# Order of the first loads in a fused attention and expert-routing kernel: first v between the k loads, blank rows in nine parts, constants in parts, rank products after the transposes

## The chip, the cores and the metric

The kernel runs on one core of a Trainium2 chip. The core has five engines with a queue of instructions each: TensorE (PE, matrix products; its weight loads are listed as PEld), VectorE (DVE), ScalarE (ACT), GpSimd (POOL) and SyncE (SP). SP only issues transfers. POOL computes and issues transfers as well. All transfers run on the core's 16 DMA engines.

The metric is the device time of one execution in microseconds (us), as a median over runs. About 0.5% (3.4 us) is what a measurement of this kernel can tell from no change.

## The reference: what is computed

Two blocks follow each other. The first is attention inside chunks of 64 positions:

```python
batch, n_heads, seq, head_dim = (8, 8, 576, 64)      # q, k, v, float32
chunk = 64
scores = scale * np.matmul(q_c, k_c.transpose(0, 1, 2, 4, 3))   # per chunk, 64 x 64
scores = scores - np.max(scores, axis=-1, keepdims=True)
attn = np.exp(scores)
attn = attn / (np.sum(attn, axis=-1, keepdims=True) + 1e-09)
out = np.matmul(attn, v_c)
```

Its output, with the heads side by side, is x: 4608 tokens of 512 numbers. The second block sends every token to one of 8 experts:

```python
logits = xn @ en.T / tau              # x and expert_emb by their norms
expert_idx = np.argmax(logits, axis=1)
gate_w = softmax(logits)[n, expert_idx[n]]
h = np.maximum(x[mask] @ w1[e], 0.0)             # w1: 8 x 512 x 1024
out[mask] = gate_w[mask, None] * (h @ w2[e])     # w2: 8 x 1024 x 512
```

## The kernel before

**Attention stage.** The 4608 tokens are 36 tiles of 128 (two chunks each). A batch of the input has 9 chunks, so it covers four and a half tiles. For each tile the kernel loads k and q (`load_qk`, line 572: `kx`, `qx`, 256 KB each), transposes them on PE (`turn_qk`, line 595), forms the scores (`scores`, line 611; DVE takes the maximum and subtracts it, lines 619 and 621), takes exp on ACT (`weights`, line 631), transposes the result (`turn_a`, line 637), and multiplies by v (`values`, line 651, tile `pv`; DVE divides by the sums, lines 659 to 662, into the row buffer `xr`, which has eight places). `turn_x` (line 680) transposes the tile's x for the router.

v is loaded by batch, with one transfer per head (`load_v`, line 584). Two buffers take turns, and `values(t)` of tile 4 is the first that reads batch 1. Chunks 0 to 3 and 4 to 8 of batch 0 are two separate calls.

**Router.** After every four tiles PE forms the logits (`logits`, line 695), transposes them back (`copy_logits`, line 710), and DVE picks the expert (`pick`, lines 724 to 728, result `eqb_all`). `place` (from line 737) counts with a few small products on PE how many earlier tokens chose the same expert (the "rank products"), and DVE makes of that a row number `dest` (lines 762 to 771). `put` (line 800) then writes a tile's rows by an indirect transfer, issued on POOL, into the table `spots` in memory. In `spots` every expert has a region; the first 4 groups of 64 rows of the first and the last expert's regions are read early, before all places are known, so they are first filled with rows that count as empty: `clear_first` (lines 549 to 556) copies the tile `blank` there.

**Expert stage.** From some 200 us on, the kernel reads groups of rows from `spots`, and PE multiplies them with w1 and w2 (lines 253, 342, 413).

**What sets the order.** The order is written out by hand: a loop over t from -3 to 38 (line 1024) works on several tiles at once, `turn_qk(t + 3)`, `scores(t + 2)`, `turn_x(t - 1)`, `values(t)`, and `load_qk(t + 7)`. Each engine executes its instructions in that order. k and q have four buffers each. k of the first four tiles is loaded on SP, all other k and all q on POOL; v and the blank rows on SP. In the built program, transfers on SP use eight completion counters in turn, so each transfer there also waits until the one eight places before it has finished. The `constants` (lines 509 to 547) are some forty small POOL instructions, all issued at the end of t = 0; `clear_first` follows at the end of t = 1, and the load of v's batch 1 in t = 2:

```python
                b = (2 * t + 2) // NCB + 1
                if b not in v_t and b < B and t > 1:
                    load_v(b)
```

Of the kernel before, what the change touches and what calls it, by code (L numbers as in the profile page):

```python
# [11 lines left out]
I32 = mybir.dt.int32  # L12
AF = mybir.ActivationFunctionType
ALU = mybir.AluOpType
# [7 lines left out]
NO_ROW = 200000  # L22
# [3 lines left out]
def kernel(  # L26
# [11 lines left out]
    nc = tc.nc  # L38
    B, H, S, Dh = q.shape
    E, D = moe_expert_emb.shape  # L40
# [13 lines left out]
    NE = 4  # L54
# [115 lines left out]
    def first_rows(s, j, n):  # L170
        r0 = (0, E - 1)[s] * R + G * j
        return spots[r0 : r0 + G * n, :]
# [273 lines left out]
    with (  # L446
# [59 lines left out]
        in_g = one.tile([P, 1], FP32, name="in_g")  # L506
        e_p = one.tile([P, 1], FP32, name="e_p")

        def constants():
            nc.gpsimd.iota(io_i, pattern=[[1, NST]], base=0, channel_multiplier=0)  # L510
            nc.gpsimd.iota(part_i, pattern=[[0, 1]], base=0, channel_multiplier=1)
            make_upper_triangular(nc, sltb, val=1.0, diag=False)
            nc.gpsimd.memset(onesb, 1.0)
            nc.gpsimd.memset(blank, 0.0)
            nc.gpsimd.memset(blank[:, D + TOK : D + TOK + 1].bitcast(I32), NO_ROW)
            nc.gpsimd.memset(ones, 1.0)
            nc.gpsimd.memset(before, 0.0)
            nc.gpsimd.memset(eqb_all[:, 0], 0.0)
            nc.gpsimd.memset(jump[:, 1], 1.0)
            nc.gpsimd.memset(nb[:, 0:1], float((SPARE + R) // G))  # L520
            nc.gpsimd.tensor_copy(io, io_i)
            nc.gpsimd.tensor_copy(at, part_i)
            nc.gpsimd.tensor_scalar(pref, io[:, 0:E], -1.0, float(E), ALU.mult, ALU.add)
            nc.gpsimd.tensor_scalar(e_base, io[:, 0:E], float(R), None, ALU.mult)
            nc.gpsimd.tensor_scalar(second, at, float(G), None, ALU.is_ge)
            nc.gpsimd.tensor_scalar(is_0, at, 2.0, None, ALU.is_lt)
            nc.gpsimd.tensor_scalar(lim, at, -float(P), float(G * NE), ALU.mult, ALU.add)
            nc.gpsimd.tensor_scalar(step, second, -2.0, 1.0, ALU.mult, ALU.add)
            nc.gpsimd.tensor_scalar(first_s, second, -1.0, 1.0, ALU.mult, ALU.add)
            nc.gpsimd.tensor_scalar(back, io, -1.0, float(NST - 1), ALU.mult, ALU.add)  # L530
            nc.gpsimd.tensor_scalar(more_g, back, float(LEAST - NE), None, ALU.is_ge)
            nc.gpsimd.tensor_scalar(pair_g, back, float(LEAST - NE), None, ALU.is_equal)
            nc.gpsimd.tensor_tensor(more_g, more_g, pair_g, ALU.add)
            nc.gpsimd.tensor_tensor(pair_g, back, more_g, ALU.subtract)
            nc.gpsimd.memset(more_e[:, NSW - 1 : NSW], 1)
            nc.gpsimd.tensor_scalar(e_0, second, float(E - 1), None, ALU.mult)
            nc.gpsimd.tensor_scalar(e_1, e_0, 1.0, None, ALU.add)
            nc.gpsimd.tensor_scalar(ends_e, io[:, 0:E], 0.0, None, ALU.is_equal)
            nc.gpsimd.tensor_scalar(full, io[:, 0:E], float(E - 1), None, ALU.is_equal)
            nc.gpsimd.tensor_tensor(ends_e, ends_e, full, ALU.add)  # L540
            nc.gpsimd.tensor_scalar(done, ends_e, float(NE), None, ALU.mult)
            nc.gpsimd.tensor_scalar(ends_e, ends_e, is_0, None, ALU.mult)
            nc.gpsimd.tensor_scalar(in_g, second, -float(G), at, ALU.mult, ALU.add)
            nc.gpsimd.tensor_scalar(e_p, second, float(R), None, ALU.mult)
            nc.gpsimd.tensor_scalar(
                base_h, io[:, 0 : E // 2], 2.0 * R, e_p, ALU.mult, ALU.add
            )

        def clear_first():

            for s in range(2):
                nc.sync.dma_start(
                    out=first_rows(s, 0, NE).rearrange("(j p) w -> p j w", p=G),
                    in_=blank[0:G].unsqueeze(1).to_broadcast([G, NE, W]),
                )
            nc.sync.dma_start(out=spots[SPARE : SPARE + G, :], in_=blank[0:G])

        before = one.tile([P, E], BF16, name="before")
# [2 lines left out]
        def load_qk(t):  # L561

            for src, nm, eng in (
                (k, "kx", nc.sync if t < 4 else nc.gpsimd),
                (q, "qx", nc.gpsimd),
            ):
                x = qk_p.tile([P, H, Dh], FP32, tag=nm, name=nm)
                done = 0
                while done < P:
                    b, s = divmod(t * P + done, S)  # L570
                    n = min(P - done, S - s)
                    eng.dma_start(  # L572
                        out=x[done : done + n],
                        in_=src[b, :, s : s + n, :].rearrange("h p d -> p h d"),
                    )
                    done += n
                qk_t[nm, t] = x.rearrange("p h d -> p (h d)")

        def load_v(b, c0=0, c1=NCB, eng=nc.sync):

            t = v_sb[b % 2]
            for h in range(H):
                r0 = CH * (h % 2)
                eng.dma_start(
                    out=t[r0 : r0 + CH, h // 2, c0:c1, 0:Dh],
                    in_=v[b, h].rearrange("(c k) d -> k c d", k=CH)[:, c0:c1],
                )
            v_t[b] = t
# [87 lines left out]
        def turn_x(t):  # L676
            d = st[t]
            ps = ps_t.tile([P, KD, P], FP32, tag="tr", name="tr")
            for c in range(KD):
                nc.tensor.transpose(ps[:, c], d["x"][:, c * P : c * P + P], ident)  # L680
            xT = wk.tile([P, KD, P], FP32, tag="xT", name="xT", bufs=RB + 1)
            nc.scalar.copy(xT, ps)  # L682
            d["xT"] = xT
            junk = one.tile([P, D], FP32, tag="junk", name="junk")
            nc.scalar.activation(
                junk, d["x"], AF.Square, accum_out=xr[:, t % NX, D + SQ : D + SQ + 1]
            )
# [20 lines left out]
        def copy_logits(b):  # L708
            n, t = sizes[b], sum(sizes[:b])
            nc.tensor.transpose(lt_ps, copied[b], ident)  # L710
            copied[b] = xr[:, t % NX : t % NX + n, D : D + E]
            nc.vector.tensor_copy(
                copied[b], lt_ps.rearrange("p (n e) -> p n e", e=Q)[:, 0:n, 0:E]
            )
# [278 lines left out]
        load_qk(1)  # L993
        for x in v_sb:
            nc.vector.memset(x[:, :, :, Dh : Dh + 1], 1.0)
        load_qk(2)
        load_qk(3)
        load_v(0, 0, 4)
        load_v(0, 4, NCB)
        norm_experts()  # L1000
        nc.gpsimd.memset(xr[:, :, D:W], 0.0)

# [18 lines left out]

        early_t = 26
        ends = {sum(sizes[: b + 1]) - 1: b for b in range(len(sizes))}
        for t in range(-3, NT + 3):

            if 0 <= t < NT:
                turn_a(t)
            if t == early_t - 1:
                count_early()
            if t + 3 < NT:  # L1030
                turn_qk(t + 3)
                if t + 7 < NT:
                    load_qk(t + 7)
            if t - 2 in ends:
                logits(ends[t - 2])
            if t == NT:
                turn_x(t - 1)
            early_parts(t, 0)
            if 0 <= t + 2 < NT:
                scores(t + 2)  # L1040
            if t - 2 in ends:
                copy_logits(ends[t - 2])
            if t - 3 in ends:
                place(ends[t - 3])
            if 0 <= t - 1 < NT - 1:
                turn_x(t - 1)
            if 0 <= t < NT:
                values(t)
                b = (2 * t + 2) // NCB + 1
                if b not in v_t and b < B and t > 1:  # L1050
                    load_v(b)
            if t == NT - 8:
                load_first(w1_sb, w1_rows)
            if t == NT - 6:
                load_first([w[0] for w in w2_sb], w2_rows)
            if 0 <= t + 2 < NT:
# [12 lines left out]
            early_parts(t, 1)  # L1069
            if t == -2:  # L1070
                turn_experts()
            if t == 0:
                constants()
            if t == 1:
                clear_first()
        groups()
        pad_places()
        put(len(to_put))
# [148 lines left out]
```

## Time and profile before

| | us |
|---|---|
| median of nine runs | 687.15 (681.52 to 690.77) |
| the profiled execution | 685.52 |
| its span | 683.7 |

| engine | busy us | share of the span |
|---|---|---|
| PE | 628.7 | 92% |
| DVE | 421.3 | 62% |
| ACT | 445.4 | 65% |
| POOL | 155.5 | 23% |

The profile is of one execution. A busy share is a mean over stages with different limits, so what a part of the kernel is worth is read from the stretch where it runs. A line of a timeline gives the start, the duration, the engine, the line of the kernel, the operation with its output and inputs, the number of instructions merged, and in brackets how long the engine had been idle before and what ended that. "issue" is a wait for nothing that the profile shows. A line of waits gives the total, how often, and the longest. A line of a stretch gives the busy time of PE, PEld, DVE, ACT and POOL (with their instructions), PE's granted clock as a share of full speed, the mean busy share of the 16 DMA engines and the rate.

Times of the product with v (`pv`, line 651) by tile: 0 at 16.34, 1 at 20.92, 2 at 24.21, 3 at 28.71, 4 at 32.01, 5 at 46.75, 6 at 50.61, 7 at 54.21, 8 at 57.87, 9 at 62.73, 11 at 70.90.

### The profile page before, as it was taken

The numbers are of one execution on the slowest core, as the hardware profiler recorded it, in microseconds if no ns is written. First come the engines' busy times: TensorE is split into PE (matmuls) and PEld (weight loads), VectorE is DVE, ScalarE is ACT, GpSimd is POOL, SyncE is SP. The second block draws the span as 40 slices with busy tenths as digits, with TensorE's granted clock in tenths as the row PEclk, the third lists the DMA queues.
The fourth block names the chain that finished last, engine by engine and source line by source line (L and its number), as shares of the span: only waits on it lengthen the run. The fifth ranks groups of instructions, "written<-read, shape, count | busy, mean of one in ns | idle before, by whom it ended". The sixth has DMA issues, their size and how long they took to land. (4 is left out here: it accounts for less than half of the span.)

```text
span 683.7 us, 24844 instructions
## 1 busy us (share of the span) xinstructions
PE 628.7 (92%) x9744; PEld 342.3 (50%) x9744; DVE 421.3 (62%) x1140; ACT 445.4 (65%) x776; POOL 155.5 (23%) x237
## 2 busy tenths in 40 slices
PE   6869898798779999999999999989999999999993
PEld 5657777686424544544544444334444444444441
DVE  4738788788369664565676556777565567564430
ACT  4626666575222767767787776878877767877650
POOL 7827676743140100100010010000100000100101
PEclk9979999999989999999999999999999999999997
DMA  9978998888936811111778111775831114411101
GB/s 258 258 185 237 256 258 263 231 245 327 343 106 227 340 57 45 49 39 44 277 261 313 49 49 41 270 290 175 331 110 42 49 46 159 172 42 33 49 30 34
DMA packets 94590, 112.66 MB, mean 165 GB/s; under 512 B 52364, under 2 KB 72588, under 8 KB 94456
## 3 DMA queue, kind: packets, MB, share of 16 engines
q1 hardware_dynamic: 82728, 72.84, 33.3%
q0 software_dynamic: 11696, 38.04, 16.8%
q8 instruction: 81, 1.33, 0.8%
q14 instruction: 53, 0.43, 0.2%
q10 hardware_dynamic: 32, 0.02, 0.0%
HBM read 334.71 MB, written 22.69 MB: 523 GB/s over the span
## 5 line engine op out<-in xcount | busy, mean ns | idle before, releaser
L413 PE MATMUL y_ps<-w,hT 128*32 128x512 f32 (+1 forms) x2368 | 272.8, 589 | 0.0
L361 ACT ACTIVATE h<-C 64x256 f32<-64x256 f32 x264 | 178.3, 675 | 95.7 <-DVE C L374 69.1
L413 PEld LDWEIGHTS y_ps<-w,hT 128*32 128x32 f32 x2368 | 87.2, 110 | 157.5 <-issue 147.4
L428 POOL DMA_INDIRECT out_dram<-y,spot x36 | 34.9, 971 | 438.0 <-ACT y L421 209.8
L374 DVE TENSOR_TENSOR C<-C,h 128x256 f32<-128x256 f32 x231 | 96.0, 416 | 49.3 <-DVEq L299 42.5
L342 PE MATMUL h<-w,S 128*32 128x256 f32 x1056 | 95.9, 379 | 0.0
L342 PE MATMUL h<-sums,xbT 128*32 128x256 f32 x1056 | 95.2, 379 | 0.0
L342 PE MATMUL h<-w,xbT 128*32 128x256 f32 x1056 | 78.6, 380 | 7.2 <-ACTq L299 6.0
L368 DVE STREAM_TRANSPOSE hT<-h 128x512 f32<-128x512 f32 x66 | 46.7, 708 | 44.0 <-ACT h L361 43.9
L342 PEld LDWEIGHTS h<-w,xbT 128*32 128x32 f32 x1056 | 40.6, 110 | 43.3 <-ACTq L299 13.4
L342 PEld LDWEIGHTS h<-w,S 128*32 128x32 f32 x1056 | 48.8, 110 | 21.8 <-ACT w L301 0.4
L342 PEld LDWEIGHTS h<-sums,xbT 128*32 128x32 f32 x1056 | 48.3, 110 | 21.9 <-ACT C L377 0.4
L227 DVE TENSOR_SCALAR rn<-rn 128x1 f32<-128x1 f32 x37 | 5.7, 153 | 68.6 <-ACT rn L224 68.6
L342 PE MATMUL h<-sums,S 128*32 128x256 f32 x528 | 47.9, 379 | 0.0
L800 POOL DMA_INDIRECT spots<-xr,dest x36 | 37.1, 1030 | 38.8 <-DVE dest L765 11.3
L682 ACT COPY xT<-tr 128x512 f32<-128x512 f32 x36 | 21.1, 587 | 37.7 <-PE tr L680 37.7
L203 DVE STREAM_TRANSPOSE xbT<-xin 128x256 f32<-128x256 f32 x73 | 44.4, 645 | 0.5 <-DVE hT L368 0.5
L224 ACT ACT_TABLE_LOAD x34 | 43.6, 1283 | 1.0 <-issue 0.3
L231 ACT ACT_TABLE_LOAD x34 | 43.6, 1283 | 0.6
L421 ACT ACTIVATE y<-y_ps,gate 128x512 f32<-128x512 f32 (+1 forms) x37 | 25.2, 682 | 24.6 <-issue 8.8
L572 POOL DMA_DIRECT2D kx<-in_k_dram x36 | 31.4, 875 | 20.7 <-PE tr L595 20.7
L651 PE MATMUL pv<-v,aT 64*64 64x65 f32 x1152 | 28.1, 227 | 8.1 <-DMA v<-in_v_dram 5.4
(202 smaller groups left out, 811.5 us busy)
## 6 DMA issues: line engine op xcount, KB each, us to landing
w<-in_moe_w_dram SPq DMA_DIRECT2D x74, 2048.0 KB
next_w<-in_moe_w_dram SPq DMA_DIRECT2D x67, 2048.0 KB
xin<-spots SPq DMA_DIRECT2D x158, 64.0 KB
qx<-in_q_dram POOLq DMA_DIRECT2D x32, 256.0 KB
v<-in_v_dram SPq DMA_DIRECT2D x56, 144.0 KB
kx<-in_k_dram POOLq DMA_DIRECT2D x28, 256.0 KB
spot<-spots SPq DMA_DIRECT2D x80, 4.0 KB
spots<-blank SPq DMA_DIRECT2D x2, 576.0 KB
```

What stands on the lines that cost most here:

```text
L203: nc.vector.transpose(xT[:, :, cols].rearrange("p c (b i) -> p b c i", i=Q), t[:, s * (D // 2) : (s + 1) * (D // 2)].rearrange("p (b i c) ...
L224: nc.scalar.activation(rn, spot[:, j % SPOTS, SQ : SQ + 1], AF.Sqrt)
L231: nc.scalar.activation(sh, sh, AF.Exp, accum_out=gate)
L342: nc.tensor.matmul(ps[t0 : t0 + Q], lhsT=a[:, c, s], rhs=w[:, r], start=c == 0, stop=c == KD // 2 - 1,)
L361: nc.scalar.activation(h[b][G * v : G * v + G, s].rearrange("p (k i) -> p k i", i=Q), x[G * s : G * s + G].rearrange("p (i k) -> p k i", i=Q),
L368: nc.vector.transpose(hT.rearrange("p k (s b i) -> p b s k i", b=2, i=Q)[:, b], h[b].rearrange("p s (k i) -> p s k i", i=Q),)
L374: nc.vector.tensor_tensor(out, a, b, op)
L413: nc.tensor.matmul(ps[Q * r : Q * r + Q, 0:w], lhsT=d["hT"][:, c, Q * t0 : Q * t0 + Q], rhs=w2_sb[s][buf_of(j)][:, c, d0 : d0 + w], start= ...
L428: ins = nc.gpsimd.indirect_dma_start(out=to, out_offset=bass.IndirectOffsetOnAxis(ap=at, axis=0), in_=y[:, 0:w], in_offset=None, bounds_ch ...
L572: eng.dma_start(out=x[done : done + n], in_=src[b, :, s : s + n, :].rearrange("h p d -> p h d"),)
L651: nc.tensor.matmul(pv[CH * c : CH * c + CH, par, i], lhsT=d["aT"][r0 : r0 + CH, i, CH * c : CH * c + CH], rhs=v_t[b][r0 : r0 + CH, i, cb, ...
L800: ins = nc.gpsimd.indirect_dma_start(out=spots, out_offset=bass.IndirectOffsetOnAxis(ap=at, axis=0), in_=m, in_offset=None, bounds_check=S ...
```

## The change

- **First loads on SP.** Before: k of tiles 0 to 3, then v's batch 0 (sixteen transfers). After: k of tiles 0 and 1, the first eight transfers of v, k of tiles 2 and 3, and then, in t = -2, the other eight of v. q stays on POOL.
- **Blank rows.** Before: two transfers of 576 KB and one of 144 KB, together. After: nine of 144 KB each, two at the end of each of t = 1 to 4 and one in t = 5.
- **v's batch 1.** It is loaded at the end of t = 1, behind two blank transfers, where it stood behind all of them. On SP the order is then: two blanks, batch 1, four blanks, batch 2 (which waits for tile 4's product), three blanks, batch 3.
- **Constants.** The same instructions, in fifteen parts, one at the end of each of t = 0 to 14; `blank` is written in the first part.
- **Rank products.** `place` is called after `turn_x(t - 1)` where it was called before it. On PE the four transposes of x now stand ahead of the rank products, once in four tiles. On DVE and ACT nothing moves.

```diff
-        def constants():
+        def constant_parts():
             nc.gpsimd.iota(io_i, pattern=[[1, NST]], base=0, channel_multiplier=0)
             nc.gpsimd.iota(part_i, pattern=[[0, 1]], base=0, channel_multiplier=1)
+            nc.gpsimd.memset(blank, 0.0)
+            nc.gpsimd.memset(blank[:, D + TOK : D + TOK + 1].bitcast(I32), NO_ROW)
+            yield
             make_upper_triangular(nc, sltb, val=1.0, diag=False)
             nc.gpsimd.memset(onesb, 1.0)
-            nc.gpsimd.memset(blank, 0.0)
-            nc.gpsimd.memset(blank[:, D + TOK : D + TOK + 1].bitcast(I32), NO_ROW)
...
+            yield
             nc.gpsimd.tensor_scalar(second, at, float(G), None, ALU.is_ge)
             nc.gpsimd.tensor_scalar(is_0, at, 2.0, None, ALU.is_lt)
+            yield
...
         def clear_first():
 
-            for s in range(2):
-                nc.sync.dma_start(
-                    out=first_rows(s, 0, NE).rearrange("(j p) w -> p j w", p=G),
-                    in_=blank[0:G].unsqueeze(1).to_broadcast([G, NE, W]),
-                )
+            for j in range(NE):
+                for s in range(2):
+                    nc.sync.dma_start(out=first_rows(s, j, 1), in_=blank[0:G])
+                    yield
             nc.sync.dma_start(out=spots[SPARE : SPARE + G, :], in_=blank[0:G])
...
         load_qk(1)
         for x in v_sb:
             nc.vector.memset(x[:, :, :, Dh : Dh + 1], 1.0)
+        load_v(0, 0, 4)
         load_qk(2)
         load_qk(3)
-        load_v(0, 0, 4)
-        load_v(0, 4, NCB)
         norm_experts()
...
+        constants, clears = constant_parts(), clear_first()
         for t in range(-3, NT + 3):
...
+            if t == -2:
+                load_v(0, 4, NCB)
             if t - 2 in ends:
                 logits(ends[t - 2])
...
+            if 0 <= t - 1 < NT - 1:
+                turn_x(t - 1)
             if t - 3 in ends:
                 place(ends[t - 3])
-            if 0 <= t - 1 < NT - 1:
-                turn_x(t - 1)
             if 0 <= t < NT:
                 values(t)
...
-            if t == 0:
-                constants()
+            if t >= 0:
+                next(constants, None)
+            if t >= 1:
+                next(clears, None)
+                next(clears, None)
             if t == 1:
-                clear_first()
+                load_v(1)
```

More of the change, by code (lines that the diff above doesn't have):

```diff
@@ L507 @@
         e_p = one.tile([P, 1], FP32, name="e_p")
-        def constants():
+        def constant_parts():
             nc.gpsimd.iota(io_i, pattern=[[1, NST]], base=0, channel_multiplier=0)
             nc.gpsimd.iota(part_i, pattern=[[0, 1]], base=0, channel_multiplier=1)
+            nc.gpsimd.memset(blank, 0.0)
+            nc.gpsimd.memset(blank[:, D + TOK : D + TOK + 1].bitcast(I32), NO_ROW)
+            yield
             make_upper_triangular(nc, sltb, val=1.0, diag=False)
             nc.gpsimd.memset(onesb, 1.0)
-            nc.gpsimd.memset(blank, 0.0)
-            nc.gpsimd.memset(blank[:, D + TOK : D + TOK + 1].bitcast(I32), NO_ROW)
-            nc.gpsimd.memset(ones, 1.0)
+            nc.gpsimd.tensor_copy(io, io_i)
+            nc.gpsimd.tensor_copy(at, part_i)
+            yield
+            nc.gpsimd.tensor_scalar(pref, io[:, 0:E], -1.0, float(E), ALU.mult, ALU.add)
+            nc.gpsimd.tensor_scalar(e_base, io[:, 0:E], float(R), None, ALU.mult)
@@ L517, in constants @@
             nc.gpsimd.memset(before, 0.0)
             nc.gpsimd.memset(eqb_all[:, 0], 0.0)
+            nc.gpsimd.memset(ones, 1.0)
+            yield
             nc.gpsimd.memset(jump[:, 1], 1.0)
             nc.gpsimd.memset(nb[:, 0:1], float((SPARE + R) // G))
[L521 to L524, printed above, removed]
+            yield
@@ L525, in constants @@
             nc.gpsimd.tensor_scalar(second, at, float(G), None, ALU.is_ge)
             nc.gpsimd.tensor_scalar(is_0, at, 2.0, None, ALU.is_lt)
+            yield
             nc.gpsimd.tensor_scalar(lim, at, -float(P), float(G * NE), ALU.mult, ALU.add)
             nc.gpsimd.tensor_scalar(step, second, -2.0, 1.0, ALU.mult, ALU.add)
+            yield
             nc.gpsimd.tensor_scalar(first_s, second, -1.0, 1.0, ALU.mult, ALU.add)
             nc.gpsimd.tensor_scalar(back, io, -1.0, float(NST - 1), ALU.mult, ALU.add)
+            yield
@@ L531, in constants @@
             nc.gpsimd.tensor_scalar(more_g, back, float(LEAST - NE), None, ALU.is_ge)
             nc.gpsimd.tensor_scalar(pair_g, back, float(LEAST - NE), None, ALU.is_equal)
+            yield
             nc.gpsimd.tensor_tensor(more_g, more_g, pair_g, ALU.add)
             nc.gpsimd.tensor_tensor(pair_g, back, more_g, ALU.subtract)
+            yield
             nc.gpsimd.memset(more_e[:, NSW - 1 : NSW], 1)
             nc.gpsimd.tensor_scalar(e_0, second, float(E - 1), None, ALU.mult)
+            yield
@@ L537, in constants @@
             nc.gpsimd.tensor_scalar(e_1, e_0, 1.0, None, ALU.add)
             nc.gpsimd.tensor_scalar(ends_e, io[:, 0:E], 0.0, None, ALU.is_equal)
+            yield
             nc.gpsimd.tensor_scalar(full, io[:, 0:E], float(E - 1), None, ALU.is_equal)
             nc.gpsimd.tensor_tensor(ends_e, ends_e, full, ALU.add)
+            yield
             nc.gpsimd.tensor_scalar(done, ends_e, float(NE), None, ALU.mult)
             nc.gpsimd.tensor_scalar(ends_e, ends_e, is_0, None, ALU.mult)
+            yield
@@ L543, in constants @@
             nc.gpsimd.tensor_scalar(in_g, second, -float(G), at, ALU.mult, ALU.add)
             nc.gpsimd.tensor_scalar(e_p, second, float(R), None, ALU.mult)
+            yield
             nc.gpsimd.tensor_scalar(
@@ L549, in clear_first @@
         def clear_first():
[L551 to L555 removed]
+            for j in range(NE):
+                for s in range(2):
+                    nc.sync.dma_start(out=first_rows(s, j, 1), in_=blank[0:G])
+                    yield
             nc.sync.dma_start(out=spots[SPARE : SPARE + G, :], in_=blank[0:G])
```

## The prediction

> **What bounds the kernel now.** I read the page first: span 683.7 us, TensorE (PE) busy 92% of it.
>
> ```profile
> span 683.7 us, 24844 instructions
> PE   6869898798779999999999999989999999999993
> ...
> PEclk9979999999989999999999999999999999999997
> DMA  9978998888936811111778111775831114411101
> ```
>
> A slice is 17.1 us. From slice 13 on PE is full at full clock: the expert stage, which the change does not touch. The first eleven slices (to 188 us) are attention, where PE and the transfers are both near full. One slice stands out, the third (34 to 51 us): PE 6, clock 7. So I went to the waits up to 180 us (total, times, longest):
>
> ```profile
> POOL kx L572 <- PE tr L595: 20.7, 10, 9.8
> ...
> DVE rs L659 <- PE pv L651: 13.1, 3, 8.2
> ACT aT L639 <- PE tr L637: 12.9, 3, 8.5
> ...
> PE pv L651 <- DMA v<-in_v_dram: 5.4, 4, 3.5
> ```
>
> Three engines wait 8 to 10 us once, and PE waits for v. The timelines say where: PE, then SP's own issues.
>
> ```profile
> 32.01 0.45 PE L651 MATMUL pv<-v,aT 64*64 64x65 f32 x12
> 33.32 0.58 PE L651 MATMUL pv<-v,aT 64*64 64x65 f32 x6 [0.85 <-issue]
> 34.96 0.48 PE L651 MATMUL pv<-v,aT 64*64 64x65 f32 x4 [1.07 <-DMA v<-in_v_dram]
> 35.63 0.48 PE L651 MATMUL pv<-v,aT 64*64 64x65 f32 x4 [0.18 <-DMA v<-in_v_dram]
> 39.66 0.48 PE L651 MATMUL pv<-v,aT 64*64 64x65 f32 x4 [3.55 <-DMA v<-in_v_dram]
> 40.76 0.48 PE L651 MATMUL pv<-v,aT 64*64 64x65 f32 x2 [0.62 <-DMA v<-in_v_dram]
> 41.17 1.11 PE L637 MATMUL tr<-ident,a 128*128 128x128 f32 x4
> ```
> ```profile
> 18.78 1.31 SPq L552 DMA_DIRECT2D spots<-blank  x2
> 20.14 2.24 SPq L556 DMA_DIRECT2D spots<-blank  x1
> 22.42 44.25 SPq L584 DMA_DIRECT2D v<-in_v_dram  x24
> ```
>
> The stalled product is tile 4's, the first to read batch 1 of v. That load stands on SP behind three blank writes (576, 576, 144 KB). In the built program a DMA on SP also waits for the one eight places before it, so the last three v loads wait for the blank writes to finish. Issued alone, the eighth starts at 30.31 and runs 2.54; its product went at 40.76. The transfers were full meanwhile (the last three columns of a stretch are PE's clock, the busy share of the DMA engines, and GB/s):
>
> ```profile
> 20.00:24.00 4.00, 3.08 (x79) 2.78 (x79) 2.62 (x6) 2.54 (x6) 3.38 (x16) 1.00 0.97 233
> 24.00:28.00 4.00, 3.12 (x79) 2.57 (x77) 2.81 (x6) 2.69 (x6) 3.43 (x10) 1.00 0.91 204
> ...
> 36.00:40.00 4.00, 0.45 (x6) 0.29 (x4) 0.00 (x0) 0.00 (x0) 0.00 (x0) 0.50 1.06 265
> ```
>
> The blank writes went first, and then v had to share with q and k of tiles 8 to 11, all issued from 25.95 on, because GpSimd (POOL) had run constants from 17.14 to 25.76.
>
> **Part 1: v's batch 1 ahead of most blank writes.** Tile 4's product starts at 32.01, tile 7's at 54.21: 22.20 us. The same four-tile stretch one batch later runs 57.87 to 70.90 (13.03), then 13.25, 13.18, 13.09: mean 13.14. So the stall, with the half clock after it (a transpose group 1.11 against 0.66), is worth 22.20 - 13.14 = **9.06 us** at most.
>
> Does v arrive? After the change SP has two blank writes (0.29 MB) and then v (1.18 MB). Blank is written on POOL right after the tile number at 17.06, so near 18.1; at 0.65 us an issue, six v loads follow by about 23.4 and the last two wait for the two blank writes. Behind the queue at the start, a v load issued 3.79 to 6.14 let its successor (eight places on) go at 11.18: 5 us from issue to landing; by that row the last v lands near 25.2 + 5 = 30. By bytes: the trace moves about 290 GB/s there; in 25.5 to 40.7 us SP's ring got about 1.6 MB (v's batch 1, 1.18 MB, and three loads of batch 2) while POOL's had 2.1 MB (tiles 8 to 11): a share of 43%, 0.125 MB/us. 1.47 MB from 18.2 us take 11.8: 30.0 us. Both come 2 us before tile 4 asks (32.01). I take no wait here, and 3 us as the far end: one load as slow as the one issued at 36.85 (3.54 us against 0.6).
>
> A rule against that: the Trainium skill, "DMA: Bandwidth & Descriptors", section "Rules for kernel authors", says to coalesce and gives 1 MiB a transfer for bandwidth; its "Anatomy" section has about 2.0 us fixed plus bytes over 436 GB/s for one DMA. If the pieces ran one after the other, my estimate from that page is nine of 2.3 us against 9 us for the three: 12 us more of SP's queue. The trace's own row is different: sixteen v loads of 64 and 80 KB went out 0.6 us apart and overlapped, at 246 to 339 GB/s in all. By the row the splitting costs six more issues, 6 x 0.65 = 3.9 us of SP.
>
> Those 3.9 us lie where SP has nothing else due: SP is idle from 43.15 to 58.24. If that cover goes, batch 2 of v is late; it is issued once tile 4 is done (33) and needed at tile 9 (62.73 now, some 54 then). With 0.59 MB of blank before it at 0.125 MB/us it lands by 44 to 46. Cost nothing, bounds 0 to 1.
>
> **Part 2: k of tiles 2 and 3 behind eight v loads (a loss).** Now tile 2's k goes out at 1.87 and its transposes run at 10.63. Then it waits behind two k and eight v issues: about 2 x 0.55 + 8 x 0.62, one of them waiting for a v: issue near 7.0. By bytes SP's ring must deliver 1.31 MB, with POOL's even share 2.6 MB in all; the windows give 2.34 MB at 10 and 2.88 at 12 us: 11.0. By the 5 us row: 12.5 to 13. PE then waits 0.4 to 2.4 us at 10.63; below nothing is excluded, since no k can be earlier than it is. PE was at half speed till 14.4 (1.06 a group); if the gap puts that off, 1.7 more. I take 1.2, bounds 0 to 4. The Trainium skill ("TensorE: Matmul & The Clock Gate", "Why this matters for your kernels") puts the gap that cools PE above about 3 us; by it the 1.7 falls away. Tile 3's k (12.9 by bytes) is due at 14.40, and v's first half, now early, was never waited for (its product waited 0.28 for ACT).
>
> **Part 3: constants in parts.** POOL's 8.6 us block goes into tiles 0 to 14 at 0.2 to 1.2 us each; POOL is busy 3.1 of some 4.2 us a tile with puts. Tile 8's k goes out near 18.5 instead of 25.95; it competes with v, as counted above. No reader is early: the first (pref, tile 5) is written in tile 2. Cost 0, bounds -0.5 to +1.
>
> **Part 4: rank products behind the transposes of x.** PE idles before L737 for 0.40 to 1.83 us in a batch:
>
> ```profile
> 66.55 0.18 PE L737 MATMUL rt_ps<-eqb_all,sltb 128*128 128x32 bf16 x1 [1.04 <-DVE eqb_all L728]
> ...
> 66.68 0.64 PE L680 MATMUL tr<-ident,xr 128*128 128x128 f32 x4
> ...
> 70.34 0.63 PE L680 MATMUL tr<-ident,xr 128*128 128x128 f32 x4 [0.32 <-issue]
> ```
>
> The 0.54 us of transposes would fill the wait, but DVE runs without a gap from 66.42 to 70.20, and the next tile's transposes (70.34) follow its last result. What is saved is lost there. I take 0; bounds -4.3 (0.54 in eight batches) and +0.5.
>
> **Part 5: the last blank writes.** Three of the nine stand behind v's batch 2, issued about 33 to 40, so out by 42 and landed by 45 to 48. The first put waits for all of them; it would be due at 53.25 - 9 = 44. POOL is in order, so tile 14's k waits too, but it has three tiles of lead. Taken: 0.4, bounds 0 to 2.
>
> **Sum.** -9.06 + 0 + 0 + 1.2 + 0 + 0 + 0.4 = -7.5 us. The profiled execution took 685.52 (span 683.7 and 1.8 around it): 678.0. The median of nine runs is 687.15, 1.6 above it: 679.6.
>
> **Rivals.**
> *Transfers bind.* Bytes are conserved: the ring was full during the stall, and afterwards (48 to 56 us) it fell to 0.33 and 0.35, which shows spare time that the change would use. For it: share 0.9 to 1.1 nearly everywhere; from 18.5 us to tile 9 (54) there are 0.6 MB left over, 4.7 of q and k (tiles 8 to 16), 1.3 of blanks, 2.4 of v and 1.2 of puts, 10.2 MB or 35 us at 290 GB/s, for 35 us. Against: 2.1 MB of these (tiles 13 to 16) are prefetch, and no k or q wait shows after 6.29 us. Half of the stall would return: 684.
> *The rank move counts.* If DVE's chain loosens, the 4.3 us come on top: 675.5.
> *Slower.* The first put. A tile's row buffer is rewritten eight tiles later, and 3.5 us pass between a put and its release (145.56 to 149.03). Tile 8 then needs its row at about 50.7, so the put may go at 47.2 at the latest. Each us that the ninth blank lands later is lost, and beyond about 47.2 + 7.9 = 55 us the kernel is slower. For it: three blanks behind eight loads that wait for PE. Against: landing estimated at 45 to 48. With landing at 60: 692.
> *Nothing happens.* v lands when it did, since bytes and not order decide: then 687 plus part 2, 688. Against: the three waits for finished blank writes.
>
> **How the numbers follow.** As summed 0.60; transfers bind 0.15; rank counts 0.10; slower 0.10; nothing happens 0.05. About 0.5% (3.4 us) is what a measurement can tell from no change. Predicted 679.6. The range takes in the rank case below, with half a microsecond more, 675.0, and above it the ends of parts 2 and 5 (2.8 and 1.6 over what I took) and the half stall: 685.5. What is left out is the slower case, that of nothing, and the far edge of the others, 0.2 together. Faster by over 0.5% (under 683.7): the sum's case, the rank case and a third of the transfers' case: 0.75. Within 0.5%: the rest of that case, and nothing (688): 0.15. Slower: 0.10.
>
> **What the profile after would show.** Right: no wait over 1 us at the product of tile 4, clock 1.00 from 32 to 46 us, tile 7's product near 46, everything later shifted by the same. Part 2: a wait of PE for k at about 10.6. Part 4: the wait before L737 shorter, the one before the next transposes as long. Wrong if PE's wait for v stands at tile 4 or comes back at tile 9, if POOL waits for blank writes beyond 48 us, or if "issue" waits of PE grow while transfers are full from 18 to 50 us.

## The result, and the profile after

| | us |
|---|---|
| before, median | 688.21 (681.52 to 692.3) |
| changed kernel, median | 681.3 (676.0 to 687.1) |
| ratio | 0.9896 (0.9871 to 0.992) |
| forecast | 679.6, a ratio of 0.989 |

The ratio, here and in the tables below, is estimated from fast runs alone (a run can fall into a slower state), and it differs from the quotient of the two medians by up to 0.2%.

The changed kernel is 1.0% faster, some 7 us. Its profiled execution took 676.73 us with a span of 675.0, against 685.52 and 683.7; it lies 4.6 us under its median, that of before 2.7 under its own, so the two profiles are 8.7 us apart. The page of it, to set beside the page of before:

```profile
span 675.0 us, 24854 instructions
...
PE   5989998987789999999999999999999999999993
...
PEclk9989999999989999999999999999999999999998
DMA  9989899979817711111787111776821114511101
```

The weak third slice is gone: PE 8 and clock 8 where 6 and 7 stood. The first slice is weaker, 5 for 6. The waits of the first 180 us (total, times, longest) name the same groups as before; the lines moved by 13 in the code:

```profile
POOL kx L585 <- PE tr L608: 17.0, 8, 5.5
...
DVE rs L672 <- PE pv L664: 7.3, 3, 3.9
PE tr L608 <- DMA kx<-in_k_dram: 6.7, 2, 3.9
```

The longest waits of POOL and DVE are about half of what they were. Below that in the list stands `PE pv L664 <- DMA v<-in_v_dram: 3.1, 4, 1.3`: PE still waits for v. The timelines of PE, and of SP's issues, show where:

```profile
13.26 0.84 PE L608 MATMUL tr<-ident,kx 128*128 128x128 f32 x4 [2.75 <-DMA kx<-in_k_dram]
...
31.88 0.56 PE L664 MATMUL pv<-v,aT 64*64 64x65 f32 x18
32.60 0.33 PE L664 MATMUL pv<-v,aT 64*64 64x65 f32 x4 [0.17 <-DMA v<-in_v_dram]
33.49 0.33 PE L664 MATMUL pv<-v,aT 64*64 64x65 f32 x4 [0.55 <-DMA v<-in_v_dram]
35.12 0.33 PE L664 MATMUL pv<-v,aT 64*64 64x65 f32 x4 [1.30 <-DMA v<-in_v_dram]
36.49 0.33 PE L664 MATMUL pv<-v,aT 64*64 64x65 f32 x2 [1.03 <-DMA v<-in_v_dram]
```
```profile
7.52 2.21 SPq L585 DMA_DIRECT2D kx<-in_k_dram  x2
9.77 6.62 SPq L597 DMA_DIRECT2D v<-in_v_dram  x8
20.61 1.19 SPq L567 DMA_DIRECT2D spots<-blank  x2
21.84 9.64 SPq L597 DMA_DIRECT2D v<-in_v_dram  x8
31.52 2.58 SPq L567 DMA_DIRECT2D spots<-blank  x4
34.20 6.73 SPq L597 DMA_DIRECT2D v<-in_v_dram  x8
40.98 1.54 SPq L567 DMA_DIRECT2D spots<-blank  x2
42.56 0.62 SPq L569 DMA_DIRECT2D spots<-blank  x1
```

Tile 4's product starts when it did, 31.88 against 32.01, and waits 3.05 us for v in four pieces instead of 5.4. The wait for the k of tile 2 at 13.26 is new.

Where the 8.7 us between the two spans lie, by the starts of the product with v:

| stretch | before | after | difference |
|---|---|---|---|
| start to tile 4 | 32.01 | 31.88 | -0.13 (tile 0 +2.34, regained by tile 3) |
| tile 4 to 7 | 22.20 | 17.68 | -4.52 |
| tile 7 to 24 | 70.50 | 69.04 | -1.46 |
| tile 24 to 35 | 48.00 | 44.07 | -3.93 |
| tile 35 to the end | 511.0 | 512.3 | +1.34 |

So only half of the 8.7 us lies where the prediction put it. The rest lies further on, where of the change only the rank products and, up to tile 14, the constants are left, and the experiments had to say whether it belongs to the change at all.

### The profile page after: what moved, and what is told of

Its sections match the earlier page's. It is cut to its first block, busy times and chain, and to the rows that moved or that the text cites. A ratio compares the mean times of both kernels' runs of the same rounds, so it can differ in the third digit from the quotient of the medians.

```text
span 675.0 us, 24854 instructions
## 1 busy us (share of the span) xinstructions
PE 625.5 (93%) x9744; PEld 355.6 (53%) x9744; DVE 422.8 (63%) x1140; ACT 445.5 (66%) x776; POOL 157.3 (23%) x237
## 3 DMA queue, kind: packets, MB, share of 16 engines
HBM read 334.71 MB, written 22.69 MB: 530 GB/s over the span
## 5 line engine op out<-in xcount | busy, mean ns | idle before, releaser
L413 PE MATMUL y_ps<-w,hT 128*32 128x512 f32 (+1 forms) x2368 | 269.1, 589 | 0.0
L413 PEld LDWEIGHTS y_ps<-w,hT 128*32 128x32 f32 x2368 | 90.1, 110 | 152.6 <-issue 145.7
L342 PE MATMUL h<-w,S 128*32 128x256 f32 x1056 | 89.5, 379 | 0.0
L342 PE MATMUL h<-sums,xbT 128*32 128x256 f32 x1056 | 89.0, 379 | 0.0
L342 PE MATMUL h<-w,xbT 128*32 128x256 f32 x1056 | 75.4, 380 | 7.2 <-ACTq L299 6.0
L203 DVE STREAM_TRANSPOSE xbT<-xin 128x256 f32<-128x256 f32 x73 | 46.1, 669 | 0.5 <-DVE hT L368 0.5
L342 PE MATMUL h<-sums,S 128*32 128x256 f32 x528 | 44.7, 379 | 0.0
L421 ACT ACTIVATE y<-y_ps,gate 128x512 f32<-128x512 f32 (+1 forms) x37 | 25.2, 681 | 22.6 <-issue 8.8
L585 POOL DMA_DIRECT2D kx<-in_k_dram x36 | 32.0, 890 | 18.1 <-PE tr L608 17.0
L585 POOL DMA_DIRECT2D qx<-in_q_dram x40 | 34.4, 865 | 0.9 <-PE tr L608 0.4
```

The source lines that it names most:

```text
L203: nc.vector.transpose(xT[:, :, cols].rearrange("p c (b i) -> p b c i", i=Q), t[:, s * (D // 2) : (s + 1) * (D // 2)].rearrange("p (b i c) ...
L342: nc.tensor.matmul(ps[t0 : t0 + Q], lhsT=a[:, c, s], rhs=w[:, r], start=c == 0, stop=c == KD // 2 - 1,)
L413: nc.tensor.matmul(ps[Q * r : Q * r + Q, 0:w], lhsT=d["hT"][:, c, Q * t0 : Q * t0 + Q], rhs=w2_sb[s][buf_of(j)][:, c, d0 : d0 + w], start= ...
L421: nc.scalar.activation(y[:, 0:w], ps[:, 0:w], AF.Copy, scale=gate_of.pop(j))
L585: eng.dma_start(out=x[done : done + n], in_=src[b, :, s : s + n, :].rearrange("h p d -> p h d"),)
```

## Experiments

Four theories run through the expectations. A: the place in SP's queue makes tile 4 wait, DVE's chain takes back what the rank products save, and the early delay is regained. B: the transfers bind, and bytes set the time. C: half of the gain is the stall, the new order of the first loads costs some 3 us, and the rank products give 2 to 4. D, formed on the results of the second group: a gain at tile 4 lasts only where the first put need not wait for blank rows. The kernels of a group below ran on one chip, beside the kernel before on that chip, which took 676.79, 675.95 and 676.65 us on these three, where it took 688 for the result.

**One part at a time (first chip).**

`v1_ahead`: the kernel before, with batch 1 of v ahead of all blank rows, and nothing else.

```diff
             if t == 1:
+                load_v(1)
                 clear_first()
```

> The kernel before with one edit: batch 1 of v is loaded at the end of tile 1, ahead of all three blank writes; nothing else moves. Theory A (the place in SP's queue made tile 4 wait): batch 1 is issued from about 16.8 us, right behind the sixteen loads of batch 0, lands before 30 us, and tile 4's product waits for v not at all or under 1 us; tile 5's product comes near 37.5 instead of 46.75 and the kernel gains 8 to 9 us (ratio 0.987). Theory B (the transfers bind, and bytes set the time): the wait shrinks to about half, since the blanks now compete with q and k instead, and the gain is 4 to 5 us (0.993).

`rank_only`: the kernel before, with `place` behind `turn_x`.

```diff
-            if t - 3 in ends:
-                place(ends[t - 3])
             if 0 <= t - 1 < NT - 1:
                 turn_x(t - 1)
+            if t - 3 in ends:
+                place(ends[t - 3])
```

> The kernel before with the rank products behind the transposes of x, and nothing else. Theory A (VectorE's chain gives the time back): the wait of PE ahead of the rank products falls from 8.0 us in all to under 4, but the wait ahead of the next tile's transposes grows by as much; ratio 1.000, within 1 us. Rival (the gap of PE was on the path): 0.5 us in each of eight batches, 3 to 4 us less, ratio 0.995.

`after_rank_back`: the changed kernel, with `place` back ahead of `turn_x`.

```diff
+            if t - 3 in ends:
+                place(ends[t - 3])
             if 0 <= t - 1 < NT - 1:
                 turn_x(t - 1)
-            if t - 3 in ends:
-                place(ends[t - 3])
```

> The changed kernel with the rank products back ahead of the transposes. Theory A: as the changed kernel, 0.990 of the kernel before, within 1 us of 681. Rival (the rank move gave what the loads did not): 0.995, some 3.5 us slower than the changed kernel.

`order_only`: the kernel before, with the new order of the first loads alone.

```diff
+        load_v(0, 0, 4)
         load_qk(2)
         load_qk(3)
-        load_v(0, 0, 4)
-        load_v(0, 4, NCB)
...
+            if t == -2:
+                load_v(0, 4, NCB)
```

> The kernel before with the new order of the first loads alone: k of tiles 0 and 1, eight loads of v, k of tiles 2 and 3, the other eight of v in t = -2. Theory A (a delay at tile 2 is paid, but the next tiles take it back while they wait for other things): PE waits 2.5 to 3 us for the k of tile 2 at about 10.5 us, tile 4's product comes within 0.5 us of 32.0, and the ratio is 1.000. Rival (the delay stays): 2 to 3 us more, 1.003 to 1.004.

| kernel | us | ratio to before on the same chip |
|---|---|---|
| v1_ahead | 669.01 | 0.9886 (0.986 to 0.9911) |
| rank_only | 675.35 | 0.997 (0.9943 to 0.9997) |
| after_rank_back | 674.82 | 0.9966 (0.9941 to 0.999) |
| order_only | 679.75 | 1.0045 (1.0021 to 1.0068) |

One added line that changes a place in a queue gives 1.1%. The timeline of PE in v1_ahead has all products of tile 4 in one piece, and SP's issues show the blank rows behind v:

```profile
30.67 0.73 PE L651 MATMUL pv<-v,aT 64*64 64x65 f32 x32
```
```profile
26.17 3.21 SPq L552 DMA_DIRECT2D spots<-blank  x2
29.42 1.82 SPq L556 DMA_DIRECT2D spots<-blank  x1
```

The kernel moves the same bytes as before in another order, and tile 4 does not wait: the order made it wait, and B falls as the cause of that wait. Tile 5 starts at 35.13 (before: 46.75).

order_only costs 0.45%, 3.0 us (1.4 to 4.6). Its PE timeline has the wait for the k of tile 2, and at tile 4 the old wait for v is still there:

```profile
13.31 1.09 PE L595 MATMUL tr<-ident,kx 128*128 128x128 f32 x4 [2.79 <-DMA kx<-in_k_dram]
...
37.39 0.48 PE L651 MATMUL pv<-v,aT 64*64 64x65 f32 x4 [3.09 <-DMA v<-in_v_dram]
...
43.59 0.90 PE L651 MATMUL pv<-v,aT 64*64 64x65 f32 x6 [0.43 <-DMA v<-in_v_dram]
```

Theory A expected tile 4 within 0.5 us of 32.0, and there it is (32.18): by then PE has made up its delay at tile 2. But A's ratio of 1.000 does not follow. The late k had also held POOL, which wrote `blank` from 20.50 (before: 18.02), and so SP, which issued the blank writes later (`21.26 1.32 SPq L552 DMA_DIRECT2D spots<-blank  x2`, before at 18.78). Batch 1 of v stands behind them, and tile 4's last product came at 43.59 for 40.76. The 3 us were lost on this way.

after_rank_back (0.9966) looks like its rival (0.995) beside the 0.9896 of the result. But the changed kernel itself was no faster on the other two chips (0.9982 and 0.9979, below), so this run says nothing about the rank products.

rank_only gives 2.0 us (0.2 to 3.9), the lower end of what C has (2 to 4), and its interval comes close to nothing. Its waits between 44 and 165 us, behind those of an unchanged kernel on the second chip (`before_again`, below):

```profile
PE rt_ps L737 <- DVE eqb_all L728: 4.8, 8, 2.8
...
PE tr L680 <- DVE xr L662: 2.1, 5, 0.6
```
```profile
PE tr L680 <- DVE xr L662: 5.8, 7, 1.0
...
PE rt_ps L737 <- DVE eqb_all L728: 0.3, 1, 0.3
```

The wait ahead of the rank products goes (4.8 to 0.3 us), and 3.7 us of it come back ahead of the next transposes.

**What stands ahead of v in the changed kernel (second chip).**

`after_v1_first`: the changed kernel, with batch 1 of v ahead of the first two blank transfers.

```diff
+            if t == 1:
+                load_v(1)
             if t >= 1:
                 next(clears, None)
                 next(clears, None)
-            if t == 1:
-                load_v(1)
```

> The changed kernel with batch 1 of v ahead of the first two blanks in tile 1, where it stood behind them. Theory C (what is left of tile 4's wait is SP sitting idle from 16.4 to 20.6 us for the blank tile, ahead of v): SP goes on with v at 16.4, the wait of 3 us at tile 4 falls under 0.5, and the kernel is 3 to 4 us faster than the changed one (ratio to the kernel before 0.985). Theory B (bytes bind): the wait at tile 4 stays at 2 to 3 us and the ratio at 0.990.

`after_v1_first_k_first`: that, and k of tiles 2 and 3 ahead of v again.

```diff
-        load_v(0, 0, 4)
         load_qk(2)
         load_qk(3)
+        load_v(0, 0, 4)
```

> As the one before it, and k of tiles 2 and 3 again ahead of the first eight loads of v. Theory C (the new order of the first loads only costs): the wait for the k of tile 2 is gone, 2 to 3 us less, ratio 0.981; faster than both kernels. Rival (the delay at tile 2 is taken back by tile 4, where nothing waits for v any more): no difference, 0.985.

`after_again` and `before_again` are the two kernels of the result, without an edit.

> The changed kernel unaltered, beside the next three. With its profile: PE waits 2 to 3 us for the k of tile 2 and about 3 us for v at tile 4. Theory C (of the changed kernel's gain about half is tile 4's stall, the new order of the first loads costs some 3 us, and the rank move gives 2 to 4): ratio 0.990, some 4 us under the one with the rank move undone (0.9966). Theory A (the rank move is worth nothing): 0.9966 again.

> The kernel before, unaltered, for a second profile of it. Ratio 1.000. Theory C: the wait for v at tile 4 is there again, 8 us between tile 4's first and last product; but the stretch from tile 5 to tile 35, 125.96 us in the first profile, is one execution's and should be nearer the 115 to 120 us of the other kernels' profiles, since what sets it is not in the change except for the rank move.

| kernel | us | ratio to before on the same chip |
|---|---|---|
| after_again | 674.57 | 0.9982 (0.9959 to 1.0006) |
| after_v1_first | 671.61 | 0.9951 (0.9927 to 0.9974) |
| after_v1_first_k_first | 673.4 | 0.9966 (0.9941 to 0.9991) |
| before_again | 676.45 | 1.0023 (0.9996 to 1.0049) |

On this chip the change is worth 0.2%, and its interval holds no change at all. Neither expectation for after_v1_first was met (0.985 or 0.990), nor that for the kernel after it (0.981 or 0.985). With v ahead of the two blank transfers the wait at tile 4 goes (first fence, PE). But the last three blank transfers stand behind batch 2, as they do in the changed kernel (second, SP), and all else is due earlier now: the first put waits for them (third, POOL), and DVE finds its row buffer still held at tiles 8 and 9 (fourth, DVE):

```profile
32.47 0.69 PE L664 MATMUL pv<-v,aT 64*64 64x65 f32 x32
```
```profile
32.82 9.98 SPq L597 DMA_DIRECT2D v<-in_v_dram  x8
42.85 1.33 SPq L567 DMA_DIRECT2D spots<-blank  x2
44.23 0.62 SPq L569 DMA_DIRECT2D spots<-blank  x1
```
```profile
50.24 1.11 POOL L813 DMA_INDIRECT spots<-xr,dest  x1 [6.77 <-DVE rs L672]
```
```profile
54.09 0.69 DVE L675 TENSOR_TENSOR xr<-pv,rs 128x512 f32<-128x512 f32 x1 [3.67 <-DMA spots<-xr,dest]
...
60.23 0.69 DVE L675 TENSOR_TENSOR xr<-pv,rs 128x512 f32<-128x512 f32 x1 [3.04 <-DMA spots<-xr,dest]
```

That is theory D. The releaser of the put's 6.77 us is named as DVE, but the row numbers that it needs were there at 43.91 (`43.72 0.18 DVE L778 TENSOR_REDUCE dest<-w 128x4 int32<-128x32 f32 x1`); what it also waits for are the blank writes, issued at 42.85 to 44.85. By the completion events in the trace the last of them landed at 49.22, and the put went 1.02 us later. With k first as well PE has no wait for the k of tile 2 (but one of 1.75 us for v at tile 4), and the put again waits: the last blank write landed at 48.36 and the put went at 49.38, again 1.02 us later. The time is no better (0.9966; the intervals overlap): where the put binds, the order of k shows no gain.

**All nine blanks early, and the best of both (third chip).**

`after_v1_nine_early`: after_v1_first, with a third blank transfer in each tile, so that all nine go out ahead of batch 2.

```diff
                 next(clears, None)
                 next(clears, None)
+                next(clears, None)
```

> The changed kernel with batch 1 of v ahead of all blanks, as in the run that lost its gain again at tiles 8 and 9, and with all nine blanks out in tiles 1 to 3 (three each), ahead of batch 2 of v. Theory D: the first put goes at about 44 us instead of 50, the waits of VectorE for puts at tiles 8 and 9 (3.67 and 3.04 us) are gone, and the ratio falls from 0.995 to 0.986 to 0.989. Theory B: the waits move elsewhere and the ratio stays at 0.995.

`v1_ahead_rank`: v1_ahead with the rank move of rank_only.

> The same with the rank products behind the transposes of x as well. If the rank move is worth 2 us (0.997 alone): 0.984 to 0.986, the fastest of all. If it is worth nothing: as the one before it, within 0.2%.

`v1_ahead_2` and `after_third` are v1_ahead and the changed kernel once more, without a further edit.

> The kernel before with batch 1 of v ahead of the three blank writes, unaltered from the first time, for a second chip and a second profile. Theory D (a gain at tile 4 lasts only where the first put need not wait for blank writes; here they are out by 31 us, well before the first put at about 43): the gain of 8 us at tile 4 is still there at tile 35, ratio 0.986 to 0.990. Theory B (bytes bind, gain is lost again whatever the order): 0.995 to 0.998 as with the changed kernel's relatives.

> The changed kernel unaltered, beside these three. It measured 0.990 on one chip and 0.998 on another. Theory D: 0.990 to 0.998, at least 5 us slower than the first three. With its profile: a wait for the k of tile 2 of 2 to 3 us, 3 to 4 us of waits for v at tile 4.

| kernel | us | ratio to before on the same chip |
|---|---|---|
| v1_ahead_2 | 670.0 | 0.9884 (0.984 to 0.9928) |
| v1_ahead_rank | 666.94 | 0.9846 (0.9801 to 0.9892) |
| after_v1_nine_early | 670.46 | 0.9905 (0.987 to 0.994) |
| after_third | 675.69 | 0.9979 (0.9948 to 1.0009) |

With the nine blanks early the first put goes at 45.81 us, 4.4 earlier than in after_v1_first, and its wait falls from 6.77 to 1.37 (timeline of POOL):

```profile
45.81 1.11 POOL L813 DMA_INDIRECT spots<-xr,dest  x1 [1.37 <-ACT aT L652]
```

The waits at tiles 8 and 9 are gone, as D had it, and the gain grows by 3.1 us (0.9951 to 0.9905 of 676; on different chips, and the intervals overlap). That is a little short of D's 0.986 to 0.989. v1_ahead repeats itself (0.9886 and 0.9884; by the medians 0.9885 and 0.9902). That its gain at tile 4 is still there at tile 35 holds in part: against before_again, which ran on another chip, the second profile of it is 12.3 us ahead at tile 5, 7.4 at tile 7 and 4.3 at tile 35, the first one 11.3 at tile 35. In after_third the wait for the k of tile 2 was 6.69 us where 2 to 3 were expected.

v1_ahead_rank is the fastest, 1.5% under before. In its profile PE waits for k and q of tile 8, 2.14 and 1.86 us (timeline of PE, for k). The two profiles of v1_ahead have no such wait, so it is not shown to be a price of v's place:

```profile
33.09 0.63 PE L595 MATMUL tr<-ident,kx 128*128 128x128 f32 x4 [2.14 <-DMA kx<-in_k_dram]
```

The constants in parts alone, and all at once in the changed kernel, were not tried.

## Why the prediction was right, and where it was not

The total was right (681.3 for 679.6, in the range, and faster as forecast), but in part by luck. By the prediction's own signs part 1 was half wrong: a wait for v stands at tile 4, with two pieces over 1 us (1.30 and 1.03), and tile 7's product came at 49.56, not near 46. Tile 4 to 7 returned 4.52 of the 9.06 us. What filled the total up lies between tile 7 and tile 35, where the prediction had nothing, and on other chips it did not come again: there the change was worth 0.2%. That the order on SP made tile 4 wait was right, and v1_ahead shows it.

**Part 1, the stall: mis-sized.** The prediction took the 9.06 us whole, by landing the last v near 25.2 + 5 = 30.2 us; tile 4's last product went at 36.49. Three steps make up these 6.3 us. The first that failed is the time of the tile `blank`, "written on POOL right after the tile number at 17.06, so near 18.1". It was done at 20.58:

```profile
14.39 0.88 POOL L585 DMA_DIRECT2D kx<-in_k_dram  x1 [3.58 <-PE tr L608]
...
17.80 0.88 POOL L585 DMA_DIRECT2D kx<-in_k_dram  x1 [1.66 <-PE tr L608]
...
19.83 0.59 POOL L512 MEMSET blank<- 128x576 f32 x1
20.48 0.10 POOL L513 MEMSET blank<- 128x1 int32 x1
```

POOL had waited for PE, and PE for k: part 2's cost passed into part 1 by way of POOL, where the prediction had added the two as if apart. SP had nothing to issue from 16.39 to 20.61, with v behind the two blanks that were not yet written. That is 2.5 us of the delay. The second step is the issues, which the prediction spread over 7.1 us from the first blank write to the last v. They took 8.8 (20.61 to 29.38), 1.7 more, and the last two were the slowest:

```profile
27.33 2.00 SPq L597 DMA_DIRECT2D v<-in_v_dram  x1
...
29.38 2.10 SPq L597 DMA_DIRECT2D v<-in_v_dram  x1
```

The third is the 5 us from issue to landing, which were 7.1 for the last load (29.38 to 36.49), 2.1 more. From 20.99 to 29.15 POOL issued q and k of tiles 8 to 10 beside these loads (from 25.95 on before); the windows (last two columns: DMA share, GB/s) have

```profile
20.00:24.00 4.00, 4.00 (x88) 3.43 (x86) 3.76 (x10) 3.50 (x8) 3.35 (x10) 1.00 0.74 181
24.00:28.00 4.00, 4.00 (x115) 3.39 (x113) 3.64 (x8) 3.39 (x8) 3.29 (x9) 1.00 1.05 296
28.00:32.00 4.00, 4.00 (x96) 3.36 (x95) 3.70 (x8) 2.78 (x8) 2.79 (x7) 1.00 1.17 308
```

The Trainium skill, "DMA: Bandwidth & Descriptors", section "Issuing engines are not separate DMA queues", says that transfers issued from different engines run on the same 16 DMA engines and interleave; these rows agree, with a share of 1.05 and 1.17 while both had transfers out. The prediction had named the competition of tile 8's k (part 3) and counted it in the rate, but not in the time of a single load. That POOL's transfers made the issues and landings longer is read from these rows and was not isolated. The wait of 3.05 us has the size of the far end that part 1 gave (3), but not its reason, one slow load. The other 1.5 us of the 4.54 that did not return lie in a stretch whose clock was 0.68 (36 to 40 us).

One reading of the kernel before was wrong, that its "last three v loads wait for the blank writes to finish", the writes eight places before them. Where such a wait takes time, SP's waits name it: up to 18 us they have `SPq L584 <- DMA v<-in_v_dram: 0.8, 2, 0.4`. From 20 to 32 us, while batch 1 was issued, they name none, and in the changed kernel none for a transfer from 20.6 to 34. What batch 1 met was its place behind the blanks, slow issues (2.54 us for the one at 30.31) and a slow landing (10.45 us for that one, 30.31 to 40.76). So the idea of transfers that bind has more in it than the prediction gave it.

The nine pieces took 5.9 us of SP's issues where the three took 3.6: 2.4 more, for 3.9 taken. The 12 us that part 1 worked out from the skill did not come; the fit in its "Anatomy" section is for transfers that GpSimd issues, and these go out on SP.

**Part 2, k behind v: mis-sized.** Taken 1.2, bounds 0 to 4. PE waited 2.75 us, and order_only measured 3.0 (1.4 to 4.6) for the reordering by itself. Tile 2's k was issued at 7.52 and used at 13.26, near the 12.5 to 13 of the prediction's own 5 us row; its 1.2 leant on the 11.0 by bytes. In the first comparison the loss looked regained by tile 3, because the kernel before had waited 1.21 and 0.88 us for nothing named at tiles 1 and 3. It was not free: in order_only it came back by way of POOL and the blank rows. How large it is varies from run to run: tile 0 starts at 18.68 to 22.69 us in the three profiles of the changed kernel, at 15.50 and 16.34 in the two of before, and their waits for k are 2.75, 2.19 and 6.69 us.

**Part 3, constants in parts: cost about 0, but not by the reason given.** POOL was not merely "busy 3.1 of some 4.2 us a tile": between puts it has a pitch, and this rose. The puts of before and after (timeline of POOL):

```profile
53.25 1.12 POOL L800 DMA_INDIRECT spots<-xr,dest  x1 [1.58 <-ACT aT L639]
...
56.52 1.06 POOL L800 DMA_INDIRECT spots<-xr,dest  x1 [0.19 <-POOL xr L668]
```
```profile
48.60 1.11 POOL L813 DMA_INDIRECT spots<-xr,dest  x1 [1.54 <-ACT aT L652]
...
52.55 1.07 POOL L813 DMA_INDIRECT spots<-xr,dest  x1 [0.19 <-ACT kxT L611]
...
89.26 1.06 POOL L813 DMA_INDIRECT spots<-xr,dest  x1 [0.18 <-issue]
...
92.44 1.05 POOL L813 DMA_INDIRECT spots<-xr,dest  x1 [0.18 <-issue]
```

3.3 us became 4.0. The last two lines settle what did it: the last part of the constants runs at 82.62, and once they have run out the pitch of the same kernel is 3.2 us again. DVE's waits for a row buffer (40 to 130 us) are 4.4 us in after_again, 4.6 in after_rank_back, 5.6 in after_third and 4.1 in nine_early, against 0.4 in before_again and 0.3 in v1_ahead; but the first profile of the changed kernel, with the same pitch, has none. That the longer pitch causes them is therefore not shown. The times leave little room for a net cost: nine_early differs from v1_ahead_2 on the same chip by the order (+3.0), the rank move (-2.0), the constants and the split blanks, and by 1.4 us in all (0.5 by the medians), which leaves 0.4 or less; the intervals are several us wide.

**Part 4, rank products: right in kind, the gain perhaps too low.** The forecast was that what is saved ahead of L737 is lost ahead of the next transposes, and the waits show it: 4.5 us saved, 3.7 lost. What it gains is 2.0 us (0.2 to 3.9) on the kernel before; on the changed kernel (0.998 with the move, 0.9966 without, on different chips) no gain is to be seen, and on v1_ahead 0.9846 against 0.9884, overlapping. Between nothing and 2 us is all that is settled; the bounds held.

**Part 5, the last blanks: right as long as part 1 failed.** The put went at 48.60, where 44 + 0.4 was expected, but 3.1 us after tile 6's product (2.6 before), so the blanks were not what bound. With v in time they are: in after_v1_first the put goes 8.4 us after tile 6's product, and 2.9 once all nine blanks are early.

**The rivals.** *Transfers bind* had the right size (half of the stall), but its rule that bytes and not order set the time is wrong: v1_ahead, v1_ahead_2 and after_v1_first move the same bytes without a wait at tile 4. *Slower by the first put* did not happen in the changed kernel, but its mechanism is real and its sum was right. It said that a row must be put by 47.2 with a gain of 9 us, and that each us after is lost. In after_v1_first tile 5 came 9.87 us earlier than before, so the limit is 46.4; the put went at 50.24, 3.8 later, and DVE waited 3.67. *Nothing happens* is what the two other chips nearly show, 0.2%, though v did land earlier there too: PE waited 3.7 us for it in after_again and 8.5 in before_again. In these two profiles tile 35 starts 2.7 us earlier with the change, and the rest of the kernel takes 2.5 us longer; one profile of each does not say whether that is chance.

**What of the total is not explained.** The stretch from tile 7 to 35 took 118.50 us in the profile of before, 113.11 in that of after, and 109.25 and 109.13 in before_again and after_again: between the last two it is equal. So the 5.4 us that the first comparison shows there are not shown to come from the change. Why the kernel before took some 12 us more for the result than on the three chips, and why the change took more of it away there, stays open. On the second and third chip the ladder reads, in us to before: v1_ahead_2 -7.8; with order, rank, constants and all nine blanks early -6.4; with the last blanks behind batch 2 -3.3; with v behind the first two blanks, which is the changed kernel, -1.2 to -1.4. By the medians the first three are -6.7, -6.2 and -4.3. The intervals of neighbouring steps overlap, so the order of the steps is better founded than their sizes.

## What to carry to other kernels

When an early load is late, first change only its place in its queue: v1_ahead, one added line, gave 1.2% (1.0% by the medians) on the chip where the whole change gave 0.2%. Costs on one chain of waits don't add as if apart: a late k held PE, PE held POOL, and POOL held the write that v's queue stood behind. Before a stall is taken out, ask what is due next once it is gone, and by when (here the ninth blank transfer, 3.8 us after its limit), and compare on several chips what is worth 1%.

## What the runs showed of the hardware

- **The clock falls after short waits too.** The Trainium skill, "TensorE: Matmul & The Clock Gate", section "Why this matters for your kernels", puts the gap that matters above about 3 us. In the changed kernel PE's granted clock (the third column from the end) was 0.69 in a stretch with one wait of 2.75 us, which may still pass as about 3. But it was also 0.68 in a stretch that followed four waits of 0.17 to 1.30 us, in which PE had been busy for 1.43 of 4.00 us; there the measurement differs from the page:

```profile
12.00:16.00 4.00, 2.75 (x41) 2.33 (x42) 0.78 (x2) 0.89 (x2) 1.61 (x2) 0.69 1.14 298
...
32.00:36.00 4.00, 1.43 (x30) 0.88 (x30) 0.81 (x2) 1.71 (x4) 0.91 (x4) 1.00 1.08 290
36.00:40.00 4.00, 3.51 (x38) 3.04 (x42) 1.75 (x4) 1.17 (x2) 1.59 (x2) 0.68 0.91 244
```

- **An issue on SP can itself be slow.** The pieces of 144 KB took 0.6 us of SP each in the changed kernel (two from 20.61 on in 1.19 us), the loads of v at 27.33 and 29.38, of the same size, 2.00 and 2.10 us, with no wait for a transfer named in SP's waits. The share of the DMA engines was 1.05 to 1.17 there; why these two were slow was not isolated.
- **One program, two times.** The kernel before took 688 us for the result and 676 on the three chips of the experiments, and the change that is worth 1.0% there was worth 0.2% on two of these. The cause is open.
